# Regrouping the diagonal score tiles and taking the block gates from fp16 parts in a one-core attention and mixer kernel

## The chip, the cores and the metric

The kernel runs on 1 core of one Trainium2 chip. The metric is the device time of one execution in microseconds, lower is better. Before the change it is 271.68 us, the median of 3 runs (271.66 to 272.45).

The engines are named as in the profile: PE multiplies matrices (PEld is its weight load), DVE is the vector engine, ACT the scalar engine, POOL is GpSimd, SP issues the transfers. Each engine works through its own list of instructions in a fixed order.

## The reference

For each of 4 batches and 8 heads there are queries, keys and values of 768 x 64. The keys are cut into 12 blocks of 64 rows. A query's gate for a block is its product with the block's mean key; it attends to the three best blocks at or before its own and to its own block, causally:

```
k_rep = k.reshape(B, H, n_blocks, block, D).mean(axis=3)
gate_scores = np.einsum('bhsd,bhnd->bhsn', q, k_rep)
gate_scores = np.where(causal, gate_scores, -1000000000.0)
top_idx = np.argsort(gate_scores, axis=-1)[..., -top_k:]
...
scores = scale * np.matmul(q, k.transpose(0, 1, 3, 2))      # masked, softmax, times v
...
x = attn_out.transpose(0, 2, 1, 3).reshape(B, S, H * D)
h = np.maximum(xt @ w_tok1, 0.0) @ w_tok2                   # xt: x with tokens and channels exchanged
u = x + h.transpose(0, 2, 1)
return u + np.maximum(u @ w_ch1, 0.0) @ w_ch2
```

The mixer after the attention has 256 hidden tokens and 1536 hidden channels over 512 channels.

## The kernel before, in words

**Attention, 16 pairs of heads.** Heads go two at a time: a pair `i` has heads `x` = 0 and 1 side by side in the 128 partitions. For each pair the transposed keys and queries are made on PE (L320), copied from PSUM to fp32 tiles `kt` and `qt` by ACT (`evac_t`, L329), and cast to fp16 by four POOL instructions (`cast`, L335: two into `KA`, two into `QA`); POOL also casts the values (L291).

The gate works in fp32: DVE sums the keys of each block (`ksum`, L343), two short reductions place the sums block-diagonally in `ks2` (`kcopy`, L351), and `gate` (L361) multiplies five 128-query slices of `qt` with the 24 columns of `ks2`. In the profile each fp32 product is two records. DVE then adds a causal bias (`gm`), takes the eight largest of 12 (L378, ten per pair), compares with the third (`lt`), makes an additive mask (`bias`, L393), PE transposes it (L404) and DVE copies it into spare partitions of `QA` (`put_mask`, L412). So the score product itself adds the mask.

**Score groups.** The lower triangle of 128 x 128 tiles of a head (21 of 36) lies in three PSUM groups, `GROUPS`: 1024, 1024 and 640 columns, two rows of key tiles each. Every group is exponentiated by one ACT instruction (`expo`, L439). Each group holds two diagonal tiles, and `diag` (L446) multiplies these two by a triangle of ones and zeros in place, 128x256 fp16, on DVE. Only for pair 0 (`TRI = 1`) is the triangle added on PE instead. `av` (L457) then does 21 products of 65 columns, the last column giving the row sum; `recip` (L465) and `norm` (L476) put the result into `x16`.

**The mixer, four batches.** When the four pairs of a batch are done, `tok1` and `umix` (L488, L500) mix tokens, `ch1` (L569) makes the hidden channels into `h2` (one buffer), with ACT and DVE applying the rectifier in 512- and 256-column parts (L579, L581). The last product is done by seven products per 2 x 2 block (`prod`, L633, named P1 to P7), with sums of operands by `hsum` on DVE (L614 to L620; tiles s1 and s3 have two buffers, s4 one) and sums of results on DVE (L648 to L669) and POOL (`vu` L655, `psum` L673, `osum` L678).

**The order.** Everything is entered as an `Op` with an engine, an estimated time, dependencies, buffers and a priority. `plan` (a list scheduler in the kernel's file) puts the operations in an order from these estimates, and the engines' lists are written out in it. Attention has the better priorities; mixer work of earlier batches is put into places where PE would be free by the estimates. So a change in an estimate or a dependency moves instructions of all engines.

Of the kernel before, what the change touches and what calls it, by code (L numbers as in the profile page):

```python
# [18 lines left out]
    (1024, [(0, 0, 768), (4, 768, 256)]),  # L19
    (1024, [(1, 0, 640), (3, 640, 384)]),  # L20
    (640, [(2, 0, 512), (5, 512, 128)]),
]
WHERE = {kk: (g, off) for g, (_, parts) in enumerate(GROUPS) for kk, off, _ in parts}
# [8 lines left out]
EARLY = 1  # L32
UVIA = 1
# [7 lines left out]
class Op:  # L41


    __slots__ = ("eng", "occ", "rec", "deps", "prio", "fn", "takes", "start", "size")

    def __init__(self, eng, occ, rec, deps, prio, fn, takes=(), size=0):
        self.eng, self.occ, self.rec, self.prio, self.fn = eng, occ, rec, prio, fn
        self.deps = [d for d in deps if d is not None]
        self.takes = takes
        self.size = size  # L50
        self.start = None

# [14 lines left out]
def plan(ops, rings, near=60.0):  # L67
# [30 lines left out]
    order = []  # L98
    left = len(ops)
    scores_left = sum(any(b.ring == "big" for b in op.takes) for op in ops)  # L100
    while left:
# [7 lines left out]
        for e, cand in ready.items():  # L109
# [7 lines left out]
            for op in cand:  # L117
                t = free[e]
                for d in op.deps:
                    t = max(t, finish(d, e))  # L120
                ok = True
# [27 lines left out]
        free[op.eng] = t + op.occ  # L149
        if op.eng in ("SP", "SPO"):  # L150
            free["SP"] = free["SPO"] = t + op.occ
# [29 lines left out]
def kernel(  # L181
# [20 lines left out]
    scale = 1.0 / (D ** 0.5)  # L202
    MASKV = -30000.0
# [9 lines left out]
                 x16=2, h1=1, u=2, uT=2, h2=1, ob=3, s1=2, s3=2, s4=1, f32=6)  # L213
# [24 lines left out]
    ks2 = [sp.tile([128, 2 * NB], FP, tag=f"ks{r}", name=f"ks{r}") for r in range(R)]  # L238
    bn16 = [sp.tile([128, NJ, 2, 64], F16, tag=f"bn{r}", name=f"bn{r}") for r in range(2)]
# [25 lines left out]
    def dve(occ, deps, prio, fn, takes=()):  # L265
        return op("DVE", occ, occ + 84, deps, prio, fn, takes)
# [56 lines left out]
    def evac_t(t32, i):  # L323
        def f():
# [4 lines left out]
            nc.scalar.copy(out=t, in_=p[:, 0:S])  # L329
        return f  # L330

    def cast(dst, name, i, x):
        def f():
            lo = 64 * x
            nc.gpsimd.tensor_copy(out=dst[i % R][x][lo:lo + 64, :], in_=T[name, i][lo:lo + 64, :])  # L335
        return f
# [54 lines left out]
    def bias(i):  # L391
        def f():
            nc.vector.scalar_tensor_tensor(  # L393
                out=bn16[i % 2][:, 1:NJ, :, 0:NB],
# [4 lines left out]
    def mask(i):  # L399
        def f():  # L400
            p = ps("bank", [128, 128 * GJ], "bps", F16)
            T["bps", i] = p
            for j in range(GJ):
                nc.tensor.transpose(out=p[:, 128 * j:128 * j + 128],  # L404
                                    in_=bn16[i % 2][:, j + 1, :, :].rearrange("p x n -> p (x n)"),
# [10 lines left out]
    def scores(i, x, g):  # L416
        def f():
            p = ps("big", None, "sps")
            T["sps", i, x, g] = p
            for kk, off, nq in GROUPS[g][1]:  # L420
                q0 = 128 * kk
                a = 0
                while a < nq:
                    n = min(nq - a, 512 - (off + a) % 512)
                    on_pe = a == 0 and i < TRI
# [8 lines left out]
    def expo(i, x, g):  # L434
        def f():
            width = GROUPS[g][0]
            e = sp.tile([128, 1024 if g < 2 else 640], F16, tag=f"e{g}", bufs=RINGS[f"e{g}"], name=f"e{g}_{i}_{x}")
# [4 lines left out]
    def diag(i, x, g):  # L442
        def f():
            step = GROUPS[g][1][1][1] // 128
            d = T["e", i, x, g].rearrange("p (a b) -> p a b", b=128)[:, 0:step + 1:step, :]
            nc.vector.tensor_tensor(out=d, in0=d, in1=m0, op=ALU.mult)  # L446
        return f

    def av(i, x):
        def f():  # L450
            p = ps("av", [128, NJ, 65], "aps")
            T["aps", i, x] = p
            for jq in range(NJ):
                for kk in range(jq + 1):
                    g, off = WHERE[kk]
                    o = off + 128 * (jq - kk)
# [262 lines left out]
    for i in range(NP):  # L719
# [9 lines left out]
        for t32, src, off in (("kl", k, 0), ("ql", q, 0.1)):  # L729
# [14 lines left out]
            for x in range(2):  # L744
                O["cast", name, i, x] = op("POOL", 770, 825, [O[name, i]] + zq + last_scores(x), pre + 4 + off,
                                           cast(dst, name, i, x))
                tb.users.append(O["cast", name, i, x])
            if name == "kt":
# [3 lines left out]
                O["kcopy", i] = dve(200, [O["ksum", i], O.get(("gate", old))], pre + 1, kcopy(i))  # L752
# [4 lines left out]
        O["v", i] = op("POOL", 800, 860, [ld] + [O.get(("av", i - R - 1, x)) for x in range(2)], pre + 8, cast_v(i))  # L757
        vb.users.append(O["v", i])
        gb = Buf("bank")
        O["gate", i] = pe(1120, [O["kcopy", i], O["qt", i]], pre + 2, gate(i), [gb])  # L760
        qb.users.append(O["gate", i])
        gs = Buf("gs")
        O["gm", i] = dve(200, [O["gate", i]], pre + 3, gm(i), [gs])
# [3 lines left out]
        O["bias", i] = dve(195, [O["lt", i], O.get(("mask", i - 2))], pre + 3, bias(i))  # L767
# [6 lines left out]
        for x in range(2):  # L774
            for g in range(3):
                pr = base + 3 * x + g
                big = Buf("big")
                occ = (434, 434, 271)[g] + (112 if i < TRI else 0)
# [5 lines left out]
                O["dg", i, x, g] = O["ex", i, x, g] if i < TRI else dve(200, [O["ex", i, x, g]], pr, diag(i, x, g))  # L784
# [20 lines left out]
    for n in range(4):  # L805
        TW.append(dve(880, W[6:10] + TW[-1:], 60.0 + 10 * n, weight_sum(n)))

    for b in range(B):
# [46 lines left out]
        for k, fc in enumerate(range(NFC)):  # L855
            for n in range(2):
                bk = Buf("bank", "big")
                O["ch1", b, fc, n] = pe((864, 436)[n], ([O["uturn", b]] if b >= UVIA else [O["uput", b, cc] for cc in range(NCC)]) + W[2:6],
# [10 lines left out]
        for j in range(3):  # L869
# [7 lines left out]
            for m in (3, 1, 2, 4):  # L877
                bf = [Buf(f"s{m}")] if m != 2 else []
                dp = {1: q21 + q22, 3: q11 + q21, 2: [sums.get(1), sums.get(3)], 4: [sums.get(2)] + q12}[m]
                sums[m] = dve(470, dp, at, hsum(b, j, m), bf)  # L880
# [24 lines left out]
            v_ = dve(420, [ka, p6], early, vsum(b, j), [fv])  # L905
# [5 lines left out]
            o11 = dve(420, [p2], early, oput(b, j, 0, 0), [ob0])  # L911
            held["a"].users.append(o11)
            p5 = product(5, "d", [], 4)
            kd = act(256, [p5], early, keep(b, j, "d"), [fd])
            p4 = product(4, "c", [kc], 5)
            vu12 = op("POOL", 660, 720, [v_], early, vu(b, j, 0, 1), [f12])
            vu21 = op("POOL", 660, 720, [v_], early, vu(b, j, 1, 0), [f21])
            vu22 = op("POOL", 660, 720, [v_], early, vu(b, j, 1, 1), [f22])
            fv.users += [vu12, vu21, vu22]
            o21 = dve(420, [p4, vu21], early, oput(b, j, 1, 0), [ob1])  # L920
# [3 lines left out]
            o12 = dve(420, [p3, vu12, o11], early, oput(b, j, 0, 1))  # L924
# [85 lines left out]
```

## Time and profile before

| | |
|---|---|
| median of 3 runs | 271.68 us |
| the profiled execution's own time | 273.09 us |
| its span, from the first to the last instruction | 271.3 us |
| granted PE clock, mean | 0.997 |
| end of the last product of attention weights and values (chain) | 165.36 us |
| end of the last PE instruction (timeline) | about 266.5 us |

In the span attention goes on until about 165 us, with mixer work of the first batch, and the beginning of the second's, between it. After that there is mixer work alone. A group's line of the profile reads: line, engine, operation, output <- inputs by name, shapes, count | busy time, mean ns of one | idle time of the engine before it and what ended it. Records of one engine overlap a little, since an instruction begins before the one ahead has fully ended: back to back on DVE, starts lie 60 to 90 ns closer than the records are long. In this text "start to start" is that spacing.

### The profile page before, as it was taken

The numbers are of one execution on the slowest core, as the hardware profiler recorded it, in microseconds if no ns is written. First come the engines' busy times: TensorE is split into PE (matmuls) and PEld (weight loads), VectorE is DVE, ScalarE is ACT, GpSimd is POOL, SyncE is SP. The second block draws the span as 40 slices with busy tenths as digits, with TensorE's granted clock in tenths as the row PEclk, the third lists the DMA queues.
The fourth block names the chain that finished last, engine by engine and source line by source line (L and its number), as shares of the span: only waits on it lengthen the run. The fifth ranks groups of instructions, "written<-read, shape, count | busy, mean of one in ns | idle before, by whom it ended". The sixth has DMA issues, their size and how long they took to land.

```text
span 271.3 us, 6571 instructions
## 1 busy us (share of the span) xinstructions
PE 257.4 (95%) x2513; PEld 194.9 (72%) x2513; DVE 196.0 (72%) x634; ACT 154.7 (57%) x224; POOL 129.9 (48%) x171
## 2 busy tenths in 40 slices
PE   8899989999989999999998999999999999999993
PEld 5788578876767777767777887656876558865882
DVE  3468948998999989699999865426943459444761
ACT  2367978867878888786767783442214432244321
POOL 8588907654624743453946524000790006920294
PEclk9999999999999999999999999999999999999998
DMA  8999999999999735847372002000692004920023
GB/s 176 200 216 220 191 210 228 227 198 175 223 218 211 174 73 117 174 97 136 118 120 77 2 21 109 29 0 0 173 218 77 2 0 145 237 86 2 0 113 121
DMA packets 94239, 34.71 MB, mean 128 GB/s; under 512 B 85568, under 2 KB 90584, under 8 KB 94208
## 3 DMA queue, kind: packets, MB, share of 16 engines
q1 hardware_dynamic: 90128, 29.89, 50.0%
q0 software_dynamic: 3360, 4.15, 9.2%
q8 instruction: 20, 0.33, 0.5%
q10 hardware_dynamic: 720, 0.25, 0.5%
q14 instruction: 11, 0.09, 0.1%
HBM read 27.21 MB, written 8.65 MB: 132 GB/s over the span
## 4 chain that ended last, share of the span: by engine, by line
PE 44%; DVE 21%; POOL 16%; DMA 9%; issue 5%; ACT 3%; SPq 1%; POOLq 0%; ACTq 0%; DVEq 0%
PE c L569 19%; PE c L633 7%; POOL vu L655 6%; DVE e L446 5%; PE sps L426 4%; DMA ql<-in_q_dram 4%; PE tok L488 3%; DMA wc<-in_moe_w_ch_dram 3%; PE aps L457 3%; DMA w<-in_moe_w_tok_dram 3%; POOL ob L678 2%; DVE Q L412 2%; POOL Q L335 2%; POOL pc L673 2%; DVE m L378 2%
## 5 line engine op out<-in xcount | busy, mean ns | idle before, releaser
L439 ACT ACTIVATE e<-sps 128x1024 f16<-128x1024 f32 (+1 forms) x96 | 84.9, 918 | 20.6 <-PE sps L426 16.9
L569 PE MATMUL c<-uT,wc 128*128 128x256 f16 (+1 forms) x384 | 67.4, 326 | 0.0
L569 PEld LDWEIGHTS <-wc 128*128 128x128 f16 x384 | 36.9, 98 | 23.4 <-issue 0.2
L426 PE MATMUL sps<-Q,KA 128*128 128x512 f16 (+3 forms) x256 | 49.7, 305 | 1.2 <-ACT e L439 0.7
L579 ACT ACTIVATE h<-c 128x512 f16<-128x512 f32 x48 | 28.7, 598 | 29.7 <-PE c L569 29.6
L335 POOL CAST KA<-kt 64x768 f16<-64x768 f32 x32 | 27.1, 847 | 38.5 <-ACT kt L329 37.4
L673 POOL TENSOR_TENSOR pc<-pc,pd 128x256 f32<-128x256 f32 x12 | 10.5, 875 | 69.9 <-ACT pd L641 69.8
L581 DVE TENSOR_SCALAR h<-c 128x256 f16<-128x256 f32 x48 | 20.2, 420 | 31.5 <-PE c L569 31.3
L446 DVE TENSOR_TENSOR e<-e,m 128x256 f16<-128x256 f16 x90 | 36.5, 412 | 7.6 <-ACT e L439 7.2
L335 POOL CAST Q<-qt 64x768 f16<-64x768 f32 x32 | 28.0, 876 | 10.9 <-ACT qt L329 9.5
L426 PEld LDWEIGHTS <-KA 128*128 128x128 f16 x256 | 23.0, 102 | 13.3 <-issue 1.3
L633 PEld LDWEIGHTS <-h 128*128 128x128 f16 x288 | 27.7, 98 | 5.3 <-issue 0.7
L457 PE MATMUL aps<-V,e 128*128 128x65 f16 x672 | 27.5, 194 | 0.9 <-DVE e L446 0.7
L457 PEld LDWEIGHTS <-e 128*128 128x128 f16 x672 | 25.9, 98 | 3.1 <-DVE e L446 1.2
L655 POOL TENSOR_TENSOR vu<-v,u 128x256 f32<-128x256 f32 x36 | 26.5, 761 | 3.3 <-DVE v L648 2.7
L633 PEld LDWEIGHTS <-s 128*128 128x128 f16 x216 | 20.9, 98 | 2.9
L361 PEld LDWEIGHTS gps<-ks,qt 128*128 128x128 f32 x160 | 19.2, 192 | 3.9 <-DVE ks L351 2.8
L361 PE MATMUL gps<-ks,qt 128*128 128x24 f32 x160 | 20.1, 268 | 1.3 <-DVE ks L351 1.2
L291 POOL CAST V<-v 128x768 f16<-128x768 f32 x16 | 13.6, 853 | 13.4 <-DMA v<-in_v_dram 12.9
L633 PE MATMUL c<-wc,h 128*128 128x256 f16 x144 | 19.6, 273 | 0.0
L633 PE MATMUL c<-wc,s 128*128 128x256 f16 x144 | 19.6, 273 | 0.0
L633 PE MATMUL c<-t,h 128*128 128x256 f16 x144 | 19.2, 273 | 0.3 <-ACT pc L641 0.3
(73 smaller groups left out, 364.7 us busy)
## 6 DMA issues: line engine op xcount, KB each, us to landing
kl<-in_k_dram SPq DMA_DIRECT2D x32, 192.0 KB, 4.8
ql<-in_q_dram SPq DMA_DIRECT2D x32, 192.0 KB, 4.4
v<-in_v_dram SPq DMA_DIRECT2D x16, 384.0 KB, 5.2
out_dram<-ob SPq DMA_DIRECT2D x24, 256.0 KB, 2.3
wc<-in_moe_w_ch_dram POOLq DMA_DIRECT2D x8, 384.0 KB, 7.4
uscr<-u SPq DMA_DIRECT2D x3, 768.0 KB, 3.7
w<-in_moe_w_tok_dram POOLq DMA_DIRECT2D x2, 384.0 KB, 7.7
KA<-indc POOLq DMA_DIRECT2D x2, 72.0 KB, 4.8
```

The source lines that it names most:

```text
L335: nc.gpsimd.tensor_copy(out=dst[i % R][x][lo:lo + 64, :], in_=T[name, i][lo:lo + 64, :])
L361: nc.tensor.matmul(out=g[:, j, :], lhsT=T["qt", i][:, 128 * j + 128:128 * j + 256], rhs=ks2[i % R], start=True, stop=True)
L426: nc.tensor.matmul(out=p[:, off + a:off + a + n], lhsT=KA[i % R][x][:, 128 * kk:128 * kk + 128], rhs=QA[i % R][x][:, q0 + a:q0 + a + n], s ...
L439: nc.scalar.activation(out=e[:, 0:width], in_=T["sps", i, x, g][:, 0:width], func=AF.Exp, scale=scale)
L446: nc.vector.tensor_tensor(out=d, in0=d, in1=m0, op=ALU.mult)
L457: nc.tensor.matmul(out=p[:, jq, :], lhsT=T["e", i, x, g][:, o:o + 128], rhs=V16[i % (R + 1)][:, x, kk, :], start=(kk == 0), stop=(kk == jq))
L569: nc.tensor.matmul(out=p, lhsT=wc1_16[:, cc, 128 * fc:128 * fc + 128], rhs=T["uT", b][:, cc, a:e], start=(cc == 0), stop=(cc == NCC - 1))
L579: nc.scalar.activation(out=T["h2", b][:, fc, a:e], in_=T["c1", b, fc, n], func=AF.Relu)
L581: nc.vector.tensor_scalar(out=T["h2", b][:, fc, a:e], in0=T["c1", b, fc, n], scalar1=0.0, scalar2=None, op0=ALU.max)
L633: nc.tensor.matmul(out=T["c2" + key, b, j], lhsT=x[:, fc, :], rhs=y[:, fc, :], start=first and fc == 0, stop=fc == HF - 1, skip_group_chec ...
L655: nc.gpsimd.tensor_tensor(out=t, in0=T["v", b, j], in1=T["u", b][:, j + 3 * row, 256 * col:256 * col + 256], op=ALU.add)
L673: return lambda: nc.gpsimd.tensor_tensor(out=T["pc", b, j], in0=T["pc", b, j], in1=T["pd", b, j], op=ALU.add)
```

## The change

1. **Score groups.** Group 0 now holds the six diagonal tiles of a head (768 columns), groups 1 and 2 the rest (1024 and 896 columns). The columns are 2688 as before; the score products are twelve per head instead of eight. `diag` is one DVE instruction of 128x768 per head, with the 128-column triangle broadcast over the tiles, and it depends on the first exponential only.
2. **Gates of pairs 2 to 15** (`SPLIT = 2`). POOL casts the whole `qt` to fp16 (`qh`, `split_q`), subtracts that from `qt` for the rest (`qr`, `rest_q`, 128x640), and copies the halves of `qh` into `QA` (`place_q`, 64x384 words of 32 bits, two per pair), in place of the two casts. DVE splits the block sums in the same way (`split_k`: two 64x12 copies into fp16 and two subtractions, in place of `kcopy`'s two reductions). The gate is then ten fp16 products of 48 columns (`gate_parts`), and `gm` becomes two DVE instructions.
3. **Numbers.** Keys and queries are scaled by 8 at the evacuation (`nc.scalar.mul` instead of `copy`), the exponent's scale divides by 64, and mask values follow.
4. **Planner.** Estimates of POOL and DVE times are changed; an operation marked `both` (`diag`, `bias`, `hsum`, `weight_sum`) is planned to start only when POOL is free, and POOL not to start within it. `ch1` of a batch depends on the last P5 of the batch ahead. Tiles s1 and s3 have one buffer instead of two; `qh` has two, `qr` one.

```diff
 GROUPS = [
-    (1024, [(0, 0, 768), (4, 768, 256)]),
-    (1024, [(1, 0, 640), (3, 640, 384)]),
-    (640, [(2, 0, 512), (5, 512, 128)]),
+    (768, [(kk, kk, 128 * kk, 128) for kk in range(6)]),
+    (1024, [(0, 1, 0, 640), (2, 3, 640, 384)]),
+    (896, [(1, 2, 0, 512), (3, 4, 512, 256), (4, 5, 768, 128)]),
 ]
...
+                if op.both:
+                    t = max(t, free["POOL"]) if t >= pool_from else t
+                elif e == "POOL" and both_from <= t < both_to:
+                    t = both_to
...
-                 x16=2, h1=1, u=2, uT=2, h2=1, ob=3, s1=2, s3=2, s4=1, f32=6)
+                 x16=2, h1=1, u=2, uT=2, h2=1, ob=3, s1=1, s3=1, s4=1, f32=6, qh=2, qr=1)
...
-            nc.scalar.copy(out=t, in_=p[:, 0:S])
+            nc.scalar.mul(out=t, in_=p[:, 0:S], mul=UP)
...
+    def split_q(i):
+            nc.gpsimd.tensor_copy(out=t, in_=T["qt", i])
+    def rest_q(i):
+            nc.gpsimd.tensor_tensor(out=t, in0=T["qt", i][:, 128:S], in1=T["qh", i][:, 128:S], op=ALU.subtract)
+    def place_q(i, x):
+            nc.gpsimd.tensor_copy(out=QA[i % R][x][lo:lo + 64, :].bitcast(FP), in_=T["qh", i][lo:lo + 64, :].bitcast(FP))
+    def split_k(i):
+            for x in range(2):
+                lo = 64 * x
+                nc.vector.tensor_copy(out=t[lo:lo + 64, 1 - x, 0, :], in_=kst[lo:lo + 64, :])
+            for x in range(2):
+                lo = 64 * x
+                nc.vector.tensor_tensor(out=t[lo:lo + 64, 1 - x, 1, :], in0=kst[lo:lo + 64, :],
+                                        in1=t[lo:lo + 64, 1 - x, 0, :], op=ALU.subtract)
+    def gate_parts(i):
+            for j in range(GJ):
+                for n, t in enumerate((T["qh", i][:, 128 * j + 128:128 * j + 256], T["qr", i][:, 128 * j:128 * j + 128])):
+                    nc.tensor.matmul(out=g[:, j].rearrange("p x c n -> p (x c n)"), lhsT=t,
+                                     rhs=kp[i % 2].rearrange("p x c n -> p (x c n)"), start=(n == 0), stop=(n == 1))
+    def gm_parts(i):
+            nc.vector.tensor_tensor(out=cut(t), in0=g[:, :, :, 1, :], in1=cut(gbias), op=ALU.add)
+            nc.vector.tensor_tensor(out=cut(t), in0=g[:, :, :, 0, :], in1=cut(t), op=ALU.add)
...
     def diag(i, x, g):
-            step = GROUPS[g][1][1][1] // 128
-            d = T["e", i, x, g].rearrange("p (a b) -> p a b", b=128)[:, 0:step + 1:step, :]
-            nc.vector.tensor_tensor(out=d, in0=d, in1=m0, op=ALU.mult)
+            d = T["e", i, x, g].rearrange("p (a b) -> p a b", b=128)
+            nc.vector.tensor_tensor(out=d, in0=d, in1=m0.broadcast_to([128, NJ, 128]), op=ALU.mult)
...
-                O["kcopy", i] = dve(200, [O["ksum", i], O.get(("gate", old))], pre + 1, kcopy(i))
+                if i < SPLIT:
+                    O["kcopy", i] = dve(200, [O["ksum", i]], pre + 1, kcopy(i))
+                else:
+                    O["kcopy", i] = dve(430, [O["ksum", i], O.get(("gate", i - 2))], pre + 1, split_k(i))
...
+            O["gate", i] = pe(330, [O["kcopy", i], O["qh", i], O["qr", i]], pre + 2, gate_parts(i), [gb])
...
-                O["dg", i, x, g] = O["ex", i, x, g] if i < TRI else dve(200, [O["ex", i, x, g]], pr, diag(i, x, g))
+                O["dg", i, x, g] = O["ex", i, x, g] if g or i < TRI else dve(470, [O["ex", i, x, g]], pr, diag(i, x, g), both=True)
...
-                O["ch1", b, fc, n] = pe((864, 436)[n], ([O["uturn", b]] if b >= UVIA else [O["uput", b, cc] for cc in range(NCC)]) + W[2:6],
+                O["ch1", b, fc, n] = pe((864, 436)[n], ([O["uturn", b]] if b >= UVIA else [O["uput", b, cc] for cc in range(NCC)]) + W[2:6] + [O.get(("p5", b - 1))],
```

## The prediction

> **What bounds the kernel now.** I read the page's busy times first, then busy times by stretch, the chain, groups by shape, and last a timeline of 20 us in mid-attention.
>
> The first line below is from the page, the next three are the stretches (start of work to 70 us, 70 to 160 us, the rest; per engine busy us and count):
>
> ```profile
> PE 257.4 (95%) x2513; PEld 194.9 (72%) x2513; DVE 196.0 (72%) x634; ACT 154.7 (57%) x224; POOL 129.9 (48%) x171
> ...
> 10.00:70.00 60.00, 56.75 (x714) 46.50 (x712) 47.62 (x189) 44.61 (x57) 37.09 (x49) 1.00 1.16 210
> 70.00:160.00 90.00, 86.09 (x951) 66.40 (x949) 83.64 (x294) 69.25 (x92) 45.20 (x54) 1.00 0.58 125
> 160.00:266.00 106.00, 105.67 (x805) 75.43 (x803) 60.57 (x134) 37.90 (x74) 38.74 (x50) 1.00 0.28 80
> ```
>
> PE is busy nearly everywhere, and at full clock. But from 70 to 160 us DVE too is busy for 83.6 of 90 us; behind 160 us it has much room. So PE sets the total, and in mid-attention DVE stands level with it. The chain says the same: from 70 to 150 us most of its pieces are DVE's, behind that PE's.
>
> Groups by shape (the busy time is the first number behind the bar, the mean in ns the second):
>
> ```profile
> L446 DVE TENSOR_TENSOR e<-e,m 128x256 f16<-128x256 f16 x90 | 36.5, 412 | 7.6 <-ACT e L439 7.2
> L457 PE MATMUL aps<-V,e 128*128 128x65 f16 x672 | 27.5, 194 | 0.9 <-DVE e L446 0.7
> L655 POOL TENSOR_TENSOR vu<-v,u 128x256 f32<-128x256 f32 x36 | 26.5, 761 | 3.3 <-DVE v L648 2.7
> L361 PE MATMUL gps<-ks,qt 128*128 128x24 f32 x160 | 20.1, 268 | 1.3 <-DVE ks L351 1.2
> L412 DVE COPY Q<-bps 12x640 f16<-12x640 f16 x32 | 15.5, 483 | 1.3 <-PE bps L404 0.3
> L351 DVE TENSOR_REDUCE ks<-kst 64x12 f32<-64x12 f32 x32 | 5.1, 159 | 0.6
> ```
>
> And the timeline (start, us, engine, line):
>
> ```profile
> 91.75 1.71 POOL L335 CAST Q<-qt 64x768 f16<-64x768 f32 x2 [0.33 <-ACT qt L329]
> 92.59 1.20 PEld L361 LDWEIGHTS gps<-ks,qt 128*128 128x128 f32 x10
> 92.65 0.95 DVE L446 TENSOR_TENSOR e<-e,m 128x256 f16<-128x256 f16 x1
> 93.52 0.82 POOL L291 CAST V<-v 128x768 f16<-128x768 f32 x1
> 93.79 0.69 DVE L446 TENSOR_TENSOR e<-e,m 128x256 f16<-128x256 f16 x1 [0.19 <-ACT e L439]
> 94.44 0.86 PEld L457 LDWEIGHTS <-e 128*128 128x128 f16 x21
> ...
> 95.77 0.28 DVE L446 TENSOR_TENSOR e<-e,m 128x256 f16<-128x256 f16 x1
> ```
>
> A triangle product takes 0.28 us while POOL rests, but 0.95 and 0.69 us here: they end 0.14 us after the casts that end at 93.46 and 94.34. DVE's instructions with two SBUF inputs wait for POOL's running instruction. The copies from PSUM (L412) and the reductions of block sums (L351, at most 0.163 us) don't, with POOL busy or not.
>
> **PE's part.** Ten gate records take 1.20 us of PE. Ten new ones have 48 fp16 columns; the nearest row are the 65-column products, 21 in 0.67 us along the chain, 0.032 us each, so 0.32 us. Bounds: none faster than 0.03 each; no slower than the 128-column fp16 ones, 0.055. I take 0.32, as their columns are nearest: 14 x 0.88 = 12.3 us saved (with the upper bound 14 x 0.65 = 9.1). Four more score products per head over the same columns add what is fixed in one, about 0.0025 us (four of 512 columns take 0.86 us, 0.215 each): 128 x 0.0025 = 0.3 us. Net, as I count all PE instructions by such spacings: 249.4 us before, 237.2 after, 12.2 less.
>
> Where it lies comes from the order in which the changed program's instructions stand. Up to the last attention-times-value product PE has 149.0 us of work before and 145.3 after; behind it 100.4 and 91.9. So the plan fills most of the freed places with mixer work, and 8.5 of the 12.2 us are gained behind the attention. Before, that product ends at 165.36 us, so 16.4 us of PE's time ahead of it is not work; behind it come 101.1 us up to PE's end at 266.5, and 4.8 us of sums and stores.
>
> **DVE's part**, ahead of the last normalisation, by start-to-start times: 90 triangle products at 0.20 become 30 of 768 columns at 0.47 (as the 768-column operand sums L616 do back to back): 18.0 to 14.1. Placing block sums, 32 at 0.08, becomes 4 of these and 56 copies and subtractions at about 0.09: +2.7. The second gate sum, 14 at 0.19: +2.7. By the order three rectifier parts (0.33) and two output sums (0.33) come ahead as well: +1.7. In sum +3.2 on 112.6 us: the triangle's saving is more than eaten, before any wait.
>
> **Waits for POOL.** Before, about 14 us: 90 x (0.412 - 0.28) = 11.7, and 2 for masks and weight differences. POOL works for 82 of the 150 us from 10 to 160, 55%. After, per pair, the two query casts (1.65) give way to one cast of all (0.83), the subtraction and two word copies (0.45 each, a cast's rate over 384 columns). The subtraction has two inputs like vu, of which one of 256 columns without a wait takes 0.67: 1.67 for 640. Bounds: 0.69 by the one-input cast, 1.67 by vu; I take 1.67, being two-input. So POOL does 1.75 us more per pair, 24.5 in all, and is busy 71%. The Trainium skill's GPSIMD Engine Reference, "Performance versus the Vector engine", gives about 2.6 cycles per element for two inputs at 1.2 GHz; 640 columns would be an estimated 1.39 us by it, 4 us less POOL time in all.
>
> A triangle product's mean wait was 0.13; scaled by 71/55 and by the longer instructions (mean remainder 0.46 instead of 0.41) it is 0.18: 30 x 0.18 = 5.4. The split of block sums is not in the trace. Its subtractions have two SBUF inputs and must wait for the copies, so POOL's next instruction can slip in between. Bounds: nothing, if POOL rests; four waits of a cast each, 3.3 us per pair, if every one meets a POOL instruction, as two sums in a row do at 192 us. I count the two subtractions alone, since the nearest rows of a one-input DVE instruction (L351, L412) don't wait: 2 x 0.71 x 0.46 = 0.65 per pair, 9 us. Masks 2, others 1. In all 17.4 against 14.
>
> Against this speaks the Trainium skill, Advanced Engine Details and Errata, "VectorE Performance Modes": one-input copies whose source and target are both in SBUF may run in a two-port mode, and these and GpSimd's instructions block each other. No row here has such a copy. By the rule the copies wait too, 1.3 us per pair, and the sum below would end 5.5 us later, near 270.5.
>
> **The sum.** DVE has 3.2 + 3.4 = 6.6 us more to do ahead of the attention's end, where PE has 3.7 less. So DVE falls behind by up to 10.3 us. About 60% of the pairs lie where DVE is full: 6.2 us, of which idle places (6.4 us from 70 to 160 are free) take perhaps 1.2; I take 5. The attention ends at 145.3 + 16.4 + 5 = 166.7. Behind it 91.9 + 0.7, and 4.8 of tail.
>
> Single buffers for s1 and s3: the sum s1 of the next block now waits for P5; s1 and the sum behind it take 0.56 each, and PE has P4, P3 and P1, 1.97 us, to cover them. Cost 0.5 us in all; bounds nothing, and 0.7 (one vu) at each of nine places, 6.3. The triangle product now follows the first of three exponentials, beside the other two, so the value products wait less (0.7 + 1.2 us on L446 in the list of waits before); this I leave in the 16.4. POOL's list also issues the eight big weight transfers. By the order the last two now stand behind the first key cast of pair 7, before behind pair 6's last query cast; the first weight difference (L600), which reads them, keeps its place on DVE between the triangles of pairs 5 and 6. Before, the last transfer was issued at 62.57, took 7.42 us and landed as DVE came to it (70.5), with DVE's whole list behind it. After, DVE has some 8.6 us of instructions between pair 7's block sum, which starts with that cast, and the difference; cast, two issues (0.76 each) and transfer are 9.8. Against them stand POOL waits on DVE's side: I take nothing, bounds 0 and 3 us. No transfer from SP is added.
>
> Scaling by 8 is one ACT instruction of the same shape: nothing, it would show at L329 (0.80).
>
> Span: 166.7 + 92.6 + 4.8 + 0.5 = 264.6, against 271.3: 6.7 us less. The profiled execution's own 273.09 lies 1.4 above the median, so I apply the difference to the median: 265.0.
>
> **Rivals.**
> - *All of PE's saving arrives* (0.25): DVE's waits fall into its idle places. For it: PE's fixed order has filler everywhere, and the triangle leaves the path. Against: DVE's 83.6 of 90. 271.7 - 12.2 + 0.5 = 260.0, from 257.5 to 262.
> - *Slower* (0.11): the split's four instructions each find POOL at work. DVE delays masks, and PE stands before scores in its fixed order. It decides once the split waits 0.65 + 6.7/(14 x 0.6) = 1.45 us per pair; at 2.0 us the time is 265.0 + 1.35 x 14 x 0.6 = 276. For it: POOL's run of six instructions is longest just when sums are ready. Against: the first cast starts with the sum (0.94 us), so POOL is often at its end.
> - *The single buffers bite* (0.12): P6 waits at each of nine places, 265.0 - 0.5 + 6.3 = 270.8.
> - *The new gates are not that cheap* (0.05): at 0.055 each, 268.2.
>
> **How the numbers follow.** Forecast 0.47, 262 to 268.5. The range takes in all but the slower rival and half a tenth below: 258.5 to 272. 0.3% is 0.8 us, about what a measurement can tell. Faster: 0.47 + 0.25 + 0.05 + 0.09 of the buffers' = 0.86; slower 0.10; same 0.04.
>
> **What would show it.** Gates: L361's successor at 0.32 us per ten. Triangle: 30 records, 0.55 while POOL rests, 0.73 in the mean. POOL busy near 154 us. Last value product near 167 us, PE's work behind it near 93. Copies of block sums at 0.16, subtractions longer. Wrong, if copies and subtractions take over 1.5 us per pair, if DVE leaves idle places between 70 and 160 us, or if PE has gaps before P6.

## The result, and the profile after

The changed kernel takes 287.73 us (median of 4, 285.78 to 291.34) against 271.75 us in the same series: ratio 1.0528, 95% interval 1.0482 to 1.0574. The highest of the four executions counts as a slow one and is left out of the ratio; the median of the other three is 286.73 us. The forecast was 265.0, range 258.5 to 272. The profiled execution's own time is 288.73 us, its span 286.3 us.

The page's busy times and granted clock, after:

```profile
PE 253.0 (88%) x2640; PEld 192.4 (67%) x2640; DVE 214.9 (75%) x616; ACT 154.3 (54%) x224; POOL 153.3 (54%) x199
...
PEclk9999799979999979999799999999999999999998
```

The stretches, after (start of work to 70 us, to 180, and the rest; per engine busy us and count, then the mean granted PE clock):

```profile
10.00:70.00 60.00, 49.22 (x666) 41.41 (x666) 47.22 (x160) 38.11 (x48) 40.70 (x54) 0.94 1.14 212
70.00:180.00 110.00, 95.90 (x1172) 74.35 (x1168) 102.69 (x313) 75.84 (x102) 68.76 (x82) 0.97 0.51 107
180.00:282.00 102.00, 99.96 (x760) 70.61 (x758) 61.73 (x127) 37.23 (x71) 35.15 (x45) 1.00 0.27 78
```

PE has idle places: 11 us before 70 us (3 before the change) and 14 from 70 to 180. In four slices of the page (about 7 us each, all ahead of 144 us) its granted clock fell to 0.7; before, every slice but the last showed 9. DVE is at 102.7 of 110 us. Behind 180 us PE is as full as ever.

Each of the four slices holds one stretch of 3.41 us at half the clock. Here are the first and the last of these, each behind the 3.41 us ahead of it (columns as above):

```profile
28.79:32.20 3.41, 0.33 (x3) 0.10 (x1) 3.40 (x15) 1.47 (x2) 3.29 (x5) 1.00 0.90 193
32.20:35.61 3.41, 3.08 (x34) 2.64 (x35) 2.27 (x6) 1.58 (x2) 3.32 (x6) 0.50 1.25 217
134.60:138.01 3.41, 0.78 (x26) 0.79 (x27) 3.28 (x8) 0.00 (x0) 2.02 (x4) 1.00 0.03 12
138.01:141.42 3.41, 3.41 (x45) 3.35 (x42) 2.15 (x15) 0.81 (x1) 0.61 (x1) 0.50 0.72 163
```

Ahead of each of the four, PE was busy for 0.33 to 1.19 of 3.41 us and DVE for 3.25 to 3.41: PE stood while DVE worked almost without a pause. Four times 3.41 us at half the clock cost at most 6.8 us.

The chain gives the end of the last value product:

```profile
184.45 1.74 PE c L638 x12
186.19 0.66 PE aps L526 x21
186.85 10.40 PE c L638 x64
```

It is 186.85 us; 166.7 was forecast. From there to the end of the span it is 99.4 us (105.9 before, 97.9 forecast). So 20.2 of the 21.7 us by which the span missed the forecast of 264.6 arose ahead of the attention's end.

Groups by shape of the instructions that the change added, after:

```profile
L516 DVE TENSOR_TENSOR e<-e,m 128x768 f16<-128x768 f16 x30 | 21.3, 717 | 2.2 <-ACT e L510 2.1
L365 POOL TENSOR_TENSOR qr<-qt,qh 128x640 f16<-128x640 f32 x14 | 20.1, 1437 | 3.5 <-PE gps L393 2.8
L383 DVE TENSOR_TENSOR kp<-kst,kp 64x12 f16<-64x12 f32 x28 | 14.8, 529 | 0.7
L380 DVE CAST kp<-kst 64x12 f16<-64x12 f32 x28 | 10.3, 368 | 0.5
```

The split of block sums (the last two rows) has 25 us of records in 56 instructions of twelve columns. A piece of the chain shows one such split:

```profile
24.95 0.82 ACT kt L345
...
25.79 0.95 DVE kst L414
...
27.25 0.26 DVE kp L380
...
27.54 0.18 DVE kp L380
...
27.74 0.78 DVE kp L383
...
28.54 2.12 DVE kp L383
...
30.67 0.82 DVE m L449 x10
...
32.20 0.28 DVE bn L464
...
32.53 0.71 PE bps L475 x5
33.24 1.49 PE sps L497 x9
```

Beside it POOL's timeline, after:

```profile
27.68 0.83 POOL L358 CAST qh<-qt 128x768 f16<-128x768 f32 x1 [0.20 <-PE sps L497]
28.45 0.82 POOL L351 CAST KA<-kt 64x768 f16<-64x768 f32 x1
29.24 1.39 POOL L365 TENSOR_TENSOR qr<-qt,qh 128x640 f16<-128x640 f32 x1
```

The two subtractions stand from 27.74 to 30.66 us: the first ends with the query cast (28.51), the second only at the end of the subtraction of queries (30.63), so it let two POOL instructions go by. Behind it in DVE's list stand the mask's maxima and `bias` (`bn`), behind those, on PE, the transposes of the mask (`bps`) and the scores. PE's list of waits shows for the whole run that DVE's late masks (`bn`, `Q`) and late triangle products (`e`) held PE up most (us in total, times, longest):

```profile
PE bps L475 <- DVE bn L464: 7.1, 5, 3.4
PE aps L526 <- DVE e L516: 5.6, 2, 4.5
...
PE sps L497 <- DVE Q L483: 2.6, 1, 2.6
```

### The profile page after: what moved, and what is told of

Its sections match the earlier page's. It is cut to its first block, busy times and chain, and to the rows that moved or that the text cites. A ratio compares the mean times of both kernels' runs of the same rounds, so it can differ in the third digit from the quotient of the medians.

```text
span 286.3 us, 6816 instructions
## 1 busy us (share of the span) xinstructions
PE 253.0 (88%) x2640; PEld 192.4 (67%) x2640; DVE 214.9 (75%) x616; ACT 154.3 (54%) x224; POOL 153.3 (54%) x199
## 4 chain that ended last, share of the span: by engine, by line
PE 43%; DVE 33%; POOL 7%; issue 5%; DMA 4%; ACT 3%; SPq 3%; POOLq 0%; DVEq 0%; ACTq 0%
PE c L638 18%; PE c L702 7%; PE sps L497 5%; PE aps L526 4%; DVE kp L383 4%; POOL vu L724 4%; DMA ql<-in_q_dram 4%; DVE e L516 3%; DVE kst L414 2%; DVE m L449 2%; DVE x L545 2%; SPq L292 2%; DVE Q L483 2%; DVE kp L380 2%; DVE u L577 2%
## 5 line engine op out<-in xcount | busy, mean ns | idle before, releaser
L510 ACT ACTIVATE e<-sps 128x768 f16<-128x768 f32 (+2 forms) x96 | 84.7, 921 | 24.1 <-PE sps L497 23.0
L497 PE MATMUL sps<-Q,KA 128*128 128x128 f16 (+3 forms) x384 | 51.7, 263 | 4.0 <-DVE Q L483 2.6
L724 POOL TENSOR_TENSOR vu<-v,u 128x256 f32<-128x256 f32 x36 | 27.8, 796 | 44.9 <-DVE v L717 44.5
L497 PEld LDWEIGHTS <-KA 128*128 128x128 f16 x384 | 29.6, 99 | 17.9 <-issue 5.7
L351 POOL CAST KA<-kt 64x768 f16<-64x768 f32 x32 | 26.9, 840 | 21.9 <-ACT kt L345 20.7
L526 PE MATMUL aps<-V,e 128*128 128x65 f16 x672 | 28.4, 198 | 7.0 <-DVE e L516 5.6
L358 POOL CAST qh<-qt 128x768 f16<-128x768 f32 x14 | 12.5, 895 | 26.9 <-ACT qt L345 26.5
L516 DVE TENSOR_TENSOR e<-e,m 128x768 f16<-128x768 f16 x30 | 21.3, 717 | 2.2 <-ACT e L510 2.1
L345 ACT ACTIVATE qt<-tql 128x768 f32<-128x768 f32 x16 | 13.0, 810 | 17.9 <-PE tql L336 17.9
L365 POOL TENSOR_TENSOR qr<-qt,qh 128x640 f16<-128x640 f32 x14 | 20.1, 1437 | 3.5 <-PE gps L393 2.8
L345 ACT ACTIVATE kt<-tkl 128x768 f32<-128x768 f32 x16 | 13.0, 810 | 13.7 <-PE tkl L336 8.6
```

The lines of the kernel that those rows point to most:

```text
L345: nc.scalar.mul(out=t, in_=p[:, 0:S], mul=UP)
L365: nc.gpsimd.tensor_tensor(out=t, in0=T["qt", i][:, 128:S], in1=T["qh", i][:, 128:S], op=ALU.subtract)
L497: nc.tensor.matmul(out=p[:, off + a:off + a + n], lhsT=KA[i % R][x][:, 128 * kk:128 * kk + 128], rhs=QA[i % R][x][:, q0 + a:q0 + a + n], s ...
L510: nc.scalar.activation(out=e[:, 0:width], in_=T["sps", i, x, g][:, 0:width], func=AF.Exp, scale=scale)
L516: nc.vector.tensor_tensor(out=d, in0=d, in1=m0.broadcast_to([128, NJ, 128]), op=ALU.mult)
L526: nc.tensor.matmul(out=p[:, jq, :], lhsT=T["e", i, x, g][:, o:o + 128], rhs=V16[i % (R + 1)][:, x, kk, :], start=(kk == 0), stop=(kk == jq))
```

## Experiments

The first theory after this reading: DVE's split of block sums waits for POOL, copies and subtractions alike, and its lateness reaches the attention's end (*waits*). The rivals: POOL's heavier list, the cast and subtraction of queries above all (*POOL*); the sheer number of DVE instructions (*DVE*); the regrouping of scores; the order that the planner wrote; and the start, where the first pairs with parts meet a pipeline that isn't full yet (*ramp*).

**Each half of the change alone.** `e1_group` is the kernel before with item 1 of the change alone (groups, twelve score products, one triangle product):

```diff
-    (1024, [(0, 0, 768), (4, 768, 256)]),
+    (768, [(kk, kk, 128 * kk, 128) for kk in range(6)]),
...
-                O["dg", i, x, g] = O["ex", i, x, g] if i < TRI else dve(200, [O["ex", i, x, g]], pr, diag(i, x, g))
+                O["dg", i, x, g] = O["ex", i, x, g] if g or i < TRI else dve(470, [O["ex", i, x, g]], pr, diag(i, x, g))
```

> The kernel before with the regrouped score tiles and the one triangle product per head alone (gates, planner's estimates, buffers as before). Split theory (the split of the block sums on DVE waits for POOL and is what costs the 16 us): 266 to 271 us, since DVE loses 3.9 us of triangle products and some 8 us of their waits. Parts theory (POOL's making of the query's parts lengthens the gate's chain): the same. Regrouping theory (twelve score products in the new groups delay PE and ACT): 273 us or more.

`e2_gates` is the changed kernel with this undone, so 90 triangle products stand beside the gates from parts:

```diff
-            nc.vector.tensor_tensor(out=d, in0=d, in1=m0.broadcast_to([128, NJ, 128]), op=ALU.mult)
+            nc.vector.tensor_tensor(out=d, in0=d, in1=m0, op=ALU.mult)
```

> The changed kernel with the old score groups and 90 triangle products, so the new gates, the split on DVE, the planner's part and the buffers without the regrouping. Split theory and parts theory: as slow as the changed kernel or slower, 287 to 297 us, since 90 triangle products wait on a POOL that is busier. Regrouping theory: 275 us or less.

Measured: `e1_group` 276.81 us, ratio to before 1.0114 [0.9995, 1.0234], which leaves open whether it differs, but isn't the gain that the split theory expected; `e2_gates` 297.21 us (its two lower executions 293.93 and 295.89), 1.0776 [1.0657, 1.0895]. The gates from parts bring the loss, and beside them the regrouping helps by some 8 us.

**The split without waits.** `e3_split_reduce` is the changed kernel in the same order of instructions; the four copies and subtractions of a pair are six reductions with one input (the rest comes from a reduction over the sum and the negated high part):

```diff
-                nc.vector.tensor_copy(out=t[lo:lo + 64, 1 - x, 0, :], in_=kst[lo:lo + 64, :])
+                nc.vector.tensor_reduce(out=t[lo:lo + 64, 1 - x, 0, :], in_=one(k2[lo:lo + 64, :, 0]), axis=AX.X, op=ALU.add)
...
+                nc.vector.tensor_reduce(out=k2[lo:lo + 64, :, 1], in_=one(t[lo:lo + 64, 1 - x, 0, :]), axis=AX.X,
+                                        op=ALU.add, negate=True)
...
-                nc.vector.tensor_tensor(out=t[lo:lo + 64, 1 - x, 1, :], in0=kst[lo:lo + 64, :],
-                                        in1=t[lo:lo + 64, 1 - x, 0, :], op=ALU.subtract)
+                nc.vector.tensor_reduce(out=t[lo:lo + 64, 1 - x, 1, :], in_=k2[lo:lo + 64], axis=AX.X, op=ALU.add)
```

> The changed kernel, with the block sums split by six short reductions of one input (a sum of one element; its negative; a sum of the two) in place of two copies and two subtractions on DVE; same values, same estimate. Reductions of this size did not wait for POOL before (0.16 us). Split theory: about 16 us of DVE's waits go, 270 to 277 us. Parts theory: the chain through POOL stays, 281 to 288 us.

Measured: 274.95 us (10 runs, 273.76 to 276.18), 1.0083 [1.0051, 1.0116]: 12.8 us less than the changed kernel's median (11.8 less than 286.73), with two more DVE instructions per pair. Its groups by shape:

```profile
L393 DVE TENSOR_REDUCE kp<-kst 64x12 f16<-64x24 f32 x28 | 4.8, 172 | 0.7
L389 DVE TENSOR_REDUCE kst<-kp 64x12 f32<-64x12 f16 x28 | 4.5, 161 | 0.9
L386 DVE TENSOR_REDUCE kp<-kst 64x12 f16<-64x12 f32 x28 | 4.3, 153 | 0.5
```

13.6 us for 84 instructions in place of 25.1 for 56; none took over 0.18 us while POOL was busy. So the waits of the split cost some 12 us of the time. But 10 us to the forecast remain.

**The split on POOL.** `e4_split_pool` takes the same four instructions from DVE to POOL:

```diff
-                nc.vector.tensor_copy(out=t[lo:lo + 64, 1 - x, 0, :], in_=kst[lo:lo + 64, :])
+                nc.gpsimd.tensor_copy(out=t[lo:lo + 64, 1 - x, 0, :], in_=kst[lo:lo + 64, :])
...
-                    O["kcopy", i] = dve(430, [O["ksum", i], O.get(("gate", i - 2))], pre + 1, split_k(i))
+                    O["kcopy", i] = op("POOL", 430, 480, [O["ksum", i], O.get(("gate", i - 2))], pre + 1, split_k(i))
```

> The changed kernel with the split's four instructions on POOL instead of DVE, the same estimate. Split theory: DVE is rid of them, 270 to 278 us, if POOL's four short instructions take about 0.5 us per pair. Parts theory: POOL's list, which the gate waits for, becomes longer, 286 to 293 us.

Measured: 278.0 us, 1.015 [1.008, 1.0221]. Up to the attention's end, at 178.1 us, DVE is busy for 134.4 us, less than before, and POOL for 77% of the time. So POOL's list can hold the attention back too, once it carries the split: in PE's list of waits the gate's wait for POOL's `qr` now stands first, with 4.9 us in five places, ahead of the mask transposes' for `bn` with 4.4.

**The planner told of the lock.** `e5_split_planned` has the changed kernel's instructions, but the planner starts a split only when POOL is free:

```diff
-                    O["kcopy", i] = dve(430, [O["ksum", i], O.get(("gate", i - 2))], pre + 1, split_k(i))
+                    O["kcopy", i] = dve(430, [O["ksum", i], O.get(("gate", i - 2))], pre + 1, split_k(i), both=True)
```

> The changed kernel with the split of block sums marked both, so that the planner's order reckons with its wait for POOL; the instructions are the same, the order is another. Waits theory (an instruction that meets POOL waits, wherever it is planned): 283 to 290 us. Plan theory (the loss is that the order did not know the wait): 274 to 279 us, as with the split that does not wait (274.95).

Measured: 284.27 us, 1.0451 [1.0372, 1.053]. The waits moved (copies now 0.524 us in the mean, subtractions 0.329) and didn't go: DVE's instructions waited 26.3 us for POOL in all, against 27.2. The planner's estimates don't fix where POOL stands when the real run comes by.

**Regrouping beside the parts, without the split's waits.** `e7_gates_reduce` is `e3_split_reduce` with the score groups of before, by the diff of `e2_gates`.

> The changed kernel with the old score groups (90 triangle products) and the split by reductions. Where DVE is full, the regrouping's saving counts: against 274.95 with the new groups, 280 to 286 us. If the regrouping is worth as little as it is beside the fp32 gates (276.8 and 272.6 against 272.3), 273 to 277 us.

Measured: 283.24 us, 1.0366 [1.0311, 1.0421], 8.3 us more than `e3_split_reduce`.

**The start.** `e8_split3` (`SPLIT = 3`) and `e11_split4_near30` (`SPLIT = 4`, planner window `near=30.0` instead of 60) are `e3_split_reduce` with one and two pairs more on fp32 gates.

```diff
-SPLIT = 2
+SPLIT = 3
```

> The split by reductions, and SPLIT = 3: pair 2 too keeps the fp32 gate and the two casts. Ramp theory (with the parts, pair 2's gate starts 5 us behind its queries instead of 1.3, and from 20 to 40 us PE has nothing else: 11.6 us of work there instead of 16.6): the 274.95 us of SPLIT = 2 fall by 2 to 4, to 271 to 273, although PE gets 0.9 us more to do. Level theory (the loss is spread over all of the attention): 275 to 277.

> As the last one with SPLIT = 4 (pairs 2 and 3 in fp32), and the planner's choice among operations that could start within 30 ns of the earliest instead of 60, without which it finds no order. Ramp theory: the whole ramp as before, some 6 us less than with SPLIT = 2: 267 to 271 us. Level theory: 275 to 278.

Measured: 283.37 us (279.06 to 283.94; too uneven for an interval) and 280.76 us, 1.0325 [1.0273, 1.0377]. Both are slower than with parts from pair 2 on, and lie above what either theory expected; fp32 gates for the first pairs brought no gain. But the order of all instructions changed with them, so two runs asked what an order alone is worth: only the planner's window was changed, in `e3_split_reduce` (`e15_near30`) and in the kernel before (`e17_before_near30`).

```diff
-def plan(ops, rings, near=60.0):
+def plan(ops, rings, near=30.0):
```

> The split by reductions with the planner's window of 30 ns instead of 60: the same instructions in another order. Order theory: it moves by 4 us or more either way from 274.95, as the runs with SPLIT = 3 and 4 did (283.4, 280.8). DVE theory: 273 to 277 us.

> The kernel before with the planner's window of 30 ns instead of 60. PE's work is the bound there and every order has fillers for it: 271 to 274 us by both theories; by 4 us or more off only if the order by itself is worth that, whatever DVE has to do.

Measured: 278.41 us, 1.0203 [1.0144, 1.0263], so 3.5 more than with the same instructions in the other order (neither expectation held); and 272.89 us, 1.0 [0.9959, 1.0041]. Order alone is worth some us in the kernel with parts, and nothing that can be measured in the kernel before. Why these orders are worse stays open.

**The rest of the change without the parts.** `e9_no_parts` keeps the regrouping, the planner's rules and the single buffers, and has fp32 gates for all pairs:

```diff
-SPLIT = 2
+SPLIT = 16
...
-            r = i % R
+            r = i
```

> The changed kernel with SPLIT = 16: all gates in fp32, no parts of queries, no split; regrouping, planner's part and single buffers stay. PE has 249.6 us of work as before. If planner and buffers cost nothing of their own, it comes out like the regrouping alone: 273 to 278 us. If they cost by themselves: over 280.

Measured: 272.55 us (10 runs), 1.0007 [0.9973, 1.0041]. Its middle stretch:

```profile
70.00:160.00 90.00, 87.33 (x1060) 70.64 (x1057) 75.10 (x257) 69.53 (x92) 46.20 (x53) 1.00 0.61 129
```

DVE is relieved by 8.5 us against before (83.64 became 75.10), and the time is the same, since PE's work is too: PE is the bound here.

**POOL's load.** In the order of `e3_split_reduce`, `e12_no_rest` has no `rest_q` and only the five gate products with `qh`:

```diff
-                for n, t in enumerate((T["qh", i][:, 128 * j + 128:128 * j + 256], T["qr", i][:, 128 * j:128 * j + 128])):
+                for n, t in enumerate((T["qh", i][:, 128 * j + 128:128 * j + 256],)):
...
-                O["qr", i] = op("POOL", 1400, 1430, [O["qh", i]], pre + 3, rest_q(i), [rb])
+                O["qr", i] = op("POOL", 1400, 1430, [O["qh", i]], pre + 3, lambda: None, [rb])
```

> The split by reductions (274.95 us), with the same order, but the rest of the queries (qr on POOL, 128x640, 1.44 us in each of 14 pairs) and its five products per pair left out: the gate is taken from the high parts of the queries alone. POOL loses 20 us of work and the gate's chain 1.4 us per pair; PE loses 2.2 us. POOL theory (what is left of the loss is POOL's extra work, as a wait of DVE and as a longer chain to the gate): 262 to 268 us. DVE theory (DVE is full by its own instructions, the second gate sum and the longer split): 271 to 274 us, little more than PE's 2.2.

and `e13_qh_act` leaves all in, with `split_q` on ACT, and so an order of its own:

```diff
-            nc.gpsimd.tensor_copy(out=t, in_=T["qt", i])
+            nc.scalar.copy(out=t, in_=T["qt", i])
```

> The split by reductions, with the high parts of the queries cast by ACT (128x768 from qt) instead of POOL; the planner is told, so the order is another. POOL loses 0.83 us per pair, ACT gains 0.80 of its quarter that is idle. POOL theory: 266 to 272 us. DVE theory: 274 to 278 us.

Measured: 270.01 us, 0.9882 [0.9804, 0.9961], and 273.09 us (10 runs), 0.9998 [0.996, 1.0035]. `e12_no_rest` lies between its two expectations. Of the 4.9 us between `e3_split_reduce` and it 1.8 are PE's own (70 products at 0.025 start to start). POOL's load up to the attention's end fell from 115.0 to 93.4 us there, about before's 86.9 again, and still the time is over 10 us behind what PE's saving would give. So POOL's load is a part, and a small one.

**DVE's load.** `e14_high_only` is `e12_no_rest`, in the same order, without the low parts of block sums: two reductions per pair instead of six, one gate sum instead of two:

```diff
-                nc.vector.tensor_reduce(out=k2[lo:lo + 64, :, 1], in_=one(t[lo:lo + 64, 1 - x, 0, :]), axis=AX.X,
-                                        op=ALU.add, negate=True)
...
-                nc.vector.tensor_reduce(out=t[lo:lo + 64, 1 - x, 1, :], in_=k2[lo:lo + 64], axis=AX.X, op=ALU.add)
...
-            nc.vector.tensor_tensor(out=cut(t), in0=g[:, :, :, 1, :], in1=cut(gbias), op=ALU.add)
-            nc.vector.tensor_tensor(out=cut(t), in0=g[:, :, :, 0, :], in1=cut(t), op=ALU.add)
+            nc.vector.tensor_tensor(out=cut(t), in0=g[:, :, :, 0, :], in1=cut(gbias), op=ALU.add)
```

> The run without the rest of the queries (270.01 us), same order, with the low parts of the block sums left out as well: two reductions per pair in place of six, one gate sum instead of two; the gate is the product of high parts alone. DVE loses about 0.55 us per pair, some 8 us, and the chain to the gate 0.4 us. DVE theory (what still holds the attention back is what DVE has more to do): 262 to 266 us. Order theory (the order was found with estimates that don't hold, and PE stands in it wherever a chain is late): 268 to 270 us.

`e18_high_planned` does the same work, with 24-column gate products, and the planner knows of it:

```diff
-            g = ps("bank", [128, GJ, 2, 2, NB], "gps")
+            g = ps("bank", [128, GJ, 2, 1, NB], "gps")
...
-            O["gate", i] = pe(330, [O["kcopy", i], O["qh", i], O["qr", i]], pre + 2, gate_parts(i), [gb])
+            O["gate", i] = pe(165, [O["kcopy", i], O["qh", i]], pre + 2, gate_parts(i), [gb])
```

> Gates from high parts alone, as e14, but with the planner told: no operation for the rest of the queries, gate products of 24 columns planned at 165 ns, the placing of block sums at 200, the gate sum at 200. If what DVE has to do is the bound, it stays at 258 to 264 us whatever the order. If the order is worth 4 us by itself, it may lie that far off 263.8.

Measured: `e14_high_only` 259.88, 261.14, 266.39 and 266.64 us in its four executions, too uneven for an interval (the median is 263.76); the profiled one is the first. `e18_high_planned` 264.19 us, 0.9661 [0.9611, 0.9711]: less than either kernel, for less work. The stretches of `e14_high_only`:

```profile
10.00:70.00 60.00, 55.31 (x757) 45.48 (x757) 47.10 (x176) 46.25 (x60) 40.04 (x57) 1.00 1.17 212
70.00:158.00 88.00, 86.86 (x1071) 67.30 (x1070) 78.95 (x262) 73.10 (x99) 49.55 (x65) 1.00 0.62 138
158.00:255.00 97.00, 93.76 (x699) 66.41 (x695) 58.78 (x120) 31.12 (x63) 35.94 (x45) 1.00 0.27 79
```

PE is full in the middle again (86.86 of 88) at full clock. The DVE work left out is 56 reductions and 14 sums; in two of the four executions most of PE's saving arrived without it. The instructions left out also stand in the chain from a pair's queries to its mask, so DVE's load and the length of that chain are not separated here: from the end of the query evacuation to the second copy of the mask it took, in the mean of 16 pairs, 7.8 us before, 14.2 in the changed kernel, 13.1 in `e3_split_reduce`, 12.6 in `e12_no_rest` and 11.4 in `e14_high_only`.

**All in one table**, counted from the traces: up to the end of the last value product (from 8 us on), how long DVE and POOL were busy, DVE's idle time, and what DVE's instructions were longer than the same ones with POOL at rest.

| kernel | time, us | attention's end | DVE busy | DVE idle | waits for POOL | POOL busy |
|---|---|---|---|---|---|---|
| before | 271.7 | 165.4 | 135.3 | 22.0 | 13.7 | 86.9 |
| changed | 287.7 | 186.9 | 153.3 | 25.6 | 27.2 | 112.6 |
| e3_split_reduce | 275.0 | 174.5 | 142.2 | 24.3 | 11.9 | 115.0 |
| e12_no_rest | 270.0 | 169.7 | 138.7 | 23.0 | 8.0 | 93.4 |
| e14_high_only (profiled 259.9) | 263.8 | 158.6 | 126.5 | 24.2 | 8.2 | 92.8 |
| e7_gates_reduce | 283.2 | 180.5 | 152.0 | 20.5 | 17.5 | 113.7 |
| e9_no_parts | 272.6 | 164.8 | 124.6 | 32.2 | 6.4 | 89.4 |
| e4_split_pool | 278.0 | 178.1 | 134.4 | 35.7 | 14.1 | 130.9 |

The changed kernel, `e3_split_reduce`, `e12_no_rest` and `e14_high_only` have one order and differ by what DVE, POOL and PE are given. In the first six rows DVE's idle time is 20 to 26 us whatever it has to do, so the attention's end moves with DVE's busy time: against before +18.0 gives +21.5, +6.9 gives +9.1, +3.4 gives +4.3, -8.8 gives -6.8. In `e9_no_parts` DVE is freed and PE's work stays; there DVE's idle time grows instead, and the end stays. `e1_group`, also with fp32 gates, is the same (DVE busy 126.3, idle 30.4, end 164.6). In the kernels with parts that are not listed, all in orders of their own, DVE's idle time is 23 to 29 us; `e15_near30` has 4.6 us more of DVE's work ahead of the attention's end than `e3_split_reduce`, and 3.7 more idle time. So the idle time is steady in one order, and less so across orders. With the split on POOL it is 35.7: there DVE's work is less than before, and PE waits for POOL.

## Why the prediction was wrong

**Right.** By the median spacings in the traces PE has 11 to 12 us less to do (12.2 forecast). Ten gate products of 48 columns take 0.25 us where nothing holds them up: less than the 0.32 taken, and below the bound of 0.03 each. The triangle product takes 0.547 us with POOL at rest (19 of them) and 0.717 in the mean (0.55 and 0.73 were forecast). POOL is busy 153.3 us (154). The single buffers, the planner's new rules and the regrouping together cost nothing that can be measured beside fp32 gates (`e9_no_parts`); apart they were not tried. Behind the attention the span is 6.5 us shorter, where 8.0 were forecast.

**Wrong, first: the size of the split.** The step was "I count the two subtractions alone, since the nearest rows of a one-input DVE instruction (L351, L412) don't wait". Those rows were of another kind: one is a reduction, the other reads PSUM. The copies from SBUF to SBUF take 0.161 us with POOL at rest (8 of them), and with POOL busy 0.450 in the mean and 1.252 at most (20). For the subtractions it is 0.166, and 0.674 and 2.124. The Trainium skill's Advanced Engine Details and Errata, "VectorE Performance Modes", which says that such copies and POOL's (GpSimd's) instructions block each other, had it right; the prediction cited it and didn't take it. Together the waits come to 16 us, 1.14 per pair, where 0.65 were taken, and DVE was busy 18.0 us longer ahead of the attention's end, where 6.6 were forecast. Besides, the four instructions start 0.2 us apart even undisturbed, not 0.09: about 0.73 us per pair instead of 0.36. The sign that the prediction named, over 1.5 us of copies and subtractions per pair, came true with 1.79 (25.1 us of records in 14 pairs). `e3_split_reduce` prices these waits at some 12 us of time. This step alone doesn't explain 287.7: with the copies' waits put in, the prediction's own sum ended near 270.5.

**Wrong, second, and hidden behind the first: how DVE's surplus becomes time.** In `e3_split_reduce` DVE has 6.9 us more to do ahead of the attention's end than before, close to the 6.6 that were forecast for the change. By the forecast's sum it should have ended near 265; it took 275. The step that failed is "About 60% of the pairs lie where DVE is full: 6.2 us, of which idle places [...] take perhaps 1.2; I take 5". In that run the mismatch is 10.6 us (PE 3.7 less, DVE 6.9 more), and it cost not 5 but 12.8 us: the attention ended at 174.5 instead of at 161.7, which is PE's work ahead of it and its idle time before. By the table DVE's idle 22 us before the change were not room. They stayed, so every us added to DVE was paid, and more than once: late masks leave PE idle, and the stretches of half the clock follow such places (the mean clock is 0.974 in the changed kernel, 0.986 in `e3_split_reduce`, 0.998 in `e14_high_only`). Ahead of the attention's end they cost at most 6.8 us in the changed kernel, 3.4 in `e3_split_reduce`, 1.7 in `e12_no_rest` and nothing in `e14_high_only`; in `e3_split_reduce` that is room enough for the 2.2 us by which 12.8 exceeds 10.6. The sum had no term for the clock, and none for the chain: from the end of a query evacuation to its gate it took 0.4 to 3.6 us before and 2.8 to 13.6 in the changed kernel (pairs 2 to 15). In one order of instructions, what is taken from DVE comes back nearly in full: 11.1 us less (the changed kernel to `e3_split_reduce`) end the attention 12.3 us earlier, 12.2 less (`e12_no_rest` to `e14_high_only`) end it 11.1 earlier. Whether that is DVE's load or the length of the chain from queries to mask is not shown.

**The rivals.** *Slower*, at 0.11, named the mechanism: the split meets POOL, masks come late, PE stands before scores. Its threshold of 1.45 us of waits per pair rested on the same 0.6, so it lay too high: at 1.14 the kernel was already 5% slower, and 1.0083 with none of these waits. *All of PE's saving arrives* (260.0) was about reached by two of the four executions of `e14_high_only` (259.88 and 261.14), which has 1.8 us less work for PE than the changed kernel and DVE's busy time 8.8 us below before. *The single buffers bite* and *the gates are not that cheap* did not happen.

**The regrouping** is worth what DVE is worth at the place: in `e9_no_parts` it is part of a relief of DVE by 10.7 us that gains nothing, since PE is the bound; beside the parts it saves 8.3 us (`e7_gates_reduce` to `e3_split_reduce`), as DVE is.

What stays open: why another order of the same instructions costs 3.5 us in the kernel with parts, why the executions of `e14_high_only` lie up to 6.8 us apart, and how the 6 us that the split on POOL still costs divide over its waits.

## What to carry to other kernels

Where two engines stand level, price what is added to either at its full length, and count an engine's idle time as room only if a run shows that it fills; taking work from one of the two helps only once the other has room too. Before moving small work to DVE beside a busy POOL, look for rows of exactly its kind (inputs and output in SBUF or not, copy or reduction): a row of another kind bounds nothing. Here the same arithmetic, written as reductions, ran without the waits and saved some 12 us.

## What the runs showed of the hardware

- A 64x12 copy from SBUF to SBUF on DVE (fp32 to fp16) took 0.161 us with POOL at rest and up to 1.252 with POOL busy; reductions of the same size over the same data, 0.153 to 0.172 in the mean, at most 0.175 with POOL busy.
- One subtraction of twelve columns took 2.124 us: it waited through two POOL instructions, so a waiting instruction doesn't always come next when the running one ends.
- The comparison `lt`, with two fp32 inputs from SBUF, waits too: 0.275 us with POOL at rest, up to 1.382. In `e3_split_reduce`, where the split no longer waits at that place, the next `lt` did (DVE's timeline):

```profile
27.25 0.34 DVE L386 TENSOR_REDUCE kp<-kst 64x12 f16<-64x12 f32 x2
27.63 0.35 DVE L389 TENSOR_REDUCE kst<-kp 64x12 f32<-64x12 f16 x2
28.01 0.36 DVE L393 TENSOR_REDUCE kp<-kst 64x12 f16<-64x24 f32 x2
...
29.23 1.62 DVE L467 TENSOR_TENSOR lt<-gm,m 128x120 f32<-128x120 f32 x1
```

- POOL's fp32 minus fp16 subtraction of 640 columns took 1.437 us; the 1.67 scaled from `vu` was too much, and the estimate of 1.39 from the Trainium skill's GPSIMD Engine Reference, "Performance versus the Vector engine", was nearer.
- A 3.41 us stretch of the changed kernel in which PE was busy for 0.33 to 1.19 us was followed, all four times, by 3.41 us at half the granted clock; in `e3_split_reduce` 1.43 us of work was followed by twice as long a stretch.
